# Sliding-window attention and a squared-ReLU feed-forward on one core: the first token group's down product formed as seven quarter products, with a new order of the whole program

## The chip, the core and the metric

The kernel runs on one NeuronCore of one Trainium2 chip. The metric is the device time of one execution in microseconds (us), smaller is better. The engines run beside each other, each through its own list of instructions in order: TensorE (PE; PEld is its weight load), VectorE (DVE), ScalarE (ACT), GpSimd (POOL) and SyncE (SP). Transfers are issued by SP, ACT and POOL and carried by 16 DMA engines.

## What is computed

```python
# attention: batch 8, heads 8, 576 positions, head dim 64, causal window of 64
scores = (1 / sqrt(64)) * q @ k.T
scores = where((rel >= 0) & (rel < 64), scores, -1e9)
attn = exp(scores - max) / (sum + 1e-9)
x = (attn @ v)  arranged as 4608 tokens x 512
# feed-forward: w_in 512 x 2048, w_out 2048 x 512
h = maximum(x @ w_in, 0)
out = (h * h) @ w_out
```

Inputs and output are 32-bit floats; on the chip the matrices are held as 16-bit floats and sums are formed in 32 bits.

## The kernel before

**Work and tiles.** Attention goes by tiles of 128 queries, 36 in all (0 to 35; the last four, 32 to 35, are the tails of two batches each). Four tiles make a group of 512 tokens, and there are nine groups. For a tile, the words of the program are: `fk`, `fq`, `fv` fetch (SP issues, 256 KB each), `kc`/`qc` or `kp`/`qp` and `vc` cast to 16 bits, `vl`/`vh` copy half tiles of v to a second layout, `T` (or `Ta`, `Tb`) transpose on TensorE with `ck`, `cq` copying the result out (tiles 0 to 7), or `tk`, `tq` transpose by DMA (tiles 8 on), `S` scores, `e` exponential on ACT, `m` mask on DVE, `V` the product with v, `n` normalization on DVE, `X` with `x` (or `dx` by DMA) the transpose of the result. `SS`, `VV` do two tiles.

**Feed-forward.** A group's hidden layer has 16 blocks of 128 columns. Groups 1 to 8 compute one block by `P` (UPm, L513: 4 matmuls 128x512), group 0 by `U` (L480: 8 matmuls 128x256, two blocks for half the tokens). Each is followed by a ReLU on ACT (`R`, `r`, L495) and a square (`Q`, `s`), whose last figure names the engine: 2 is ACT (L506), 1 is DVE (L510).

**Down product.** Groups 1 to 8 use seven products of quarters instead of eight (out_seven, L662): the hidden layer is cut by tokens and by blocks in four quarters, w_out likewise, and sums of quarters are multiplied. `hs` g.i.half forms the sums of the hidden layer on DVE (L676, 8 per group, 128x1024), `ws` kind.k the sums of w_out (L521, 16 once, on DVE, into `wb_all` and, kind 3, into w_out itself), `Z` g.n.half is half a product (8 matmuls 128x256, L696), `ev` g.n takes a product out of PSUM: n = 0 on ACT (L728), n = 1 to 6 on DVE (L730). Products 0 and 1 share a PSUM bank, 3 and 5, and 4 and 6; `sd` stores. Group 0 alone uses the plain form: `O` ts.fq, 4 matmuls 128x512 (L647), four such for each of four token tiles, `oe` copies out (two on ACT, two on DVE), `st` stores:

```python
    def O(ts, fq):
        if fq == 0:
            ops_of[ts] = psum_of("out")
        for f in range(4 * fq, 4 * fq + 4):
            nc.tensor.matmul(
                ops_of[ts][:], h2s[0][:, f, ts * P:(ts + 1) * P], w_out_sb[:, f, :],
                start=(f == 0), stop=(f == FFC - 1))
```

**Weights.** `fw` j loads a quarter of the columns of w_in (L203), `fo` j a quarter of the rows of w_out (L208). Both are issued by POOL, cast to 16 bits under way, and stand in POOL's list between its casts. Blocks 4j to 4j+3 use quarter j of both: `U` p.f2 needs quarter f2 // 2 of w_in; product 0 of the seven needs rows 0 and 1 of the quarters of w_out (half 0 the first, half 1 the second), product 1 quarters 2 and 3, and `ws` kind.0 and kind.1 quarters 0 and 2, kind.2 and kind.3 quarters 1 and 3.

**The order.** No scheduler places anything: the string ORDER (L16) lists some 1,270 words, and each engine gets its instructions in that order, with waits only where data or buffers ask for them. `W` n puts n matmuls on zeros into TensorE's list (L350, results unused). Buffers that matter: 14 stage buffers for fetched tiles, two PSUM banks called up (`ps_u`) and two called out (`ps_o`), which `U` takes in turn, `P` from up, `O` and `Z` from out; two buffers for the hidden layer (one group each), one `hs_all` for two of the four sums.

Of the kernel before, what the change touches and what calls it, by code (L numbers as in the profile page):

```python
# [33 lines left out]
fq13 r1.9 VV4 s1.9.2 qp12.0 P1.12 fv13 r1.2 n8 st3 O1.2 s1.2.1 r1.12 fk14 s1.12.2 hs1.0.0 X8 fq14
P1.4 x8.2 vc12.0 n9 P1.7 vh12.0 r1.4 hs1.1.0 s1.4.2 O1.3 kp13.0 h10 r1.7 tk12 hs1.2.0 Z1.0.0 oe1.2
s1.7.1 SS5 fv14 hs1.0.1 qp13.0 Z1.0.1 e11 st1 hs1.1.1 Z1.2.0 fk15 vc13.0 ev1.0 m11 fq15 e10 vl13.0
Z1.1.0 hs1.2.1 vh13.0 Z1.1.1 tq12 hs1.3.0 kp14.0 X9 ev1.1 Z1.2.1 m10 qp14.0 fv15 x9.2 hs1.3.1
Z1.3.0 fk16 ev1.2 VV5 Z1.4.0 n10 vc14.0 Z1.4.1 n11 vh14.0 X10 vl14.0 X11 x10.1 Z1.3.1 kp15.0 x11.1
P2.7 tk14 ev1.3 qp15.0 P2.10 ev1.4 r2.7 fq16 s2.7.2 SS6 r2.10 P2.8 fv16 e12 vc15.0 s2.10.1 Z1.5.0
tq14 vl15.0 r2.8 m12 P2.4 e13 kp16.0 s2.8.1 fk17 Z1.5.1 r2.4 m13 fq17 s2.4.2 P2.6 ev1.5 qp16.0 h14  # L40
P2.2 sd1.0 r2.6 fv17 s2.6.2 P2.11 vc16.0 fk18 r2.2 vh16.0 VV6 r2.11 P2.0 s2.2.2 s2.11.1 n12 P2.13
r2.0 kp17.0 n13 s2.0.2 P2.3 tk16 qp17.0 r2.13 SS7 r2.3 s2.13.1 dx12 Z1.6.0 e14 s2.3.1 P2.15 e15
m14 fq18 P2.5 vc17.0 r2.15 m15 tq16 s2.15.2 vl17.0 P2.1 r2.5 vh17.0 VV7 s2.5.2 fv18 kp18.0 P2.12
r2.1 n15 fk19 s2.1.2 P2.9 n14 r2.12 Z2.0.0 s2.12.1 r2.9 dx14 s2.9.1 Z2.0.1 qp18.0 hs2.0.0 fq19
Z1.6.1 ev2.0 hs2.2.0 P2.14 fv19 ev1.6 SS8 r2.14 hs2.1.0 vc18.0 sd1.1 Z2.1.0 e16 fk20 vh18.0
s2.14.1 Z2.2.0 fq20 kp19.0 e17 hs2.0.1 vl18.0 Z2.1.1 hs2.1.1 tk18 P3.14 hs2.2.1 ev2.1 qp19.0 fv20
m17 Z2.3.0 r3.14 tq18 m16 s3.14.2 P3.1 vc19.0 hs2.3.0 vl19.0 VV8 r3.1 fk21 hs2.3.1 Z2.2.1 fq21
s3.1.1 Z2.3.1 n16 kp20.0 P3.5 ev2.2 qp20.0 P3.0 ev2.3 r3.5 n17 s3.5.2 Z2.5.0 r3.0 h18 dx16 P3.12
s3.0.2 vc20.0 P3.11 r3.12 fv21 vh20.0 s3.12.1 Z2.4.0 fk22 r3.11 s3.11.1 Z2.5.1 kp21.0 P3.8 ev2.5
tk20 SS9 qp21.0 r3.8 P3.10 s3.8.2 tq20 e18 P3.9 r3.10 Z2.4.1 m18 sd2.0 vc21.0 s3.10.2 fq22 P3.2  # L50
r3.9 vh21.0 ev2.4 e19 vl21.0 P3.7 fv22 kp22.0 r3.2 m19 Z2.6.0 s3.2.2 VV9 r3.7 s3.9.2 P3.3 n19
s3.7.2 P3.13 n18 r3.3 s3.3.2 P3.6 dx18 r3.13 hs3.0.0 SS10 r3.6 s3.13.1 qp22.0 Z3.0.0 fk23 e20
s3.6.1 fq23 P3.4 e21 vc22.0 hs3.1.0 Z2.6.1 vl22.0 m20 r3.4 vh22.0 s3.4.1 P3.15 ev2.6 Z3.0.1 r3.15
hs3.2.0 sd2.1 Z3.2.0 fv23 kp23.0 ev3.0 m21 fk24 P4.13 s3.15.1 qp23.0 tk22 hs3.0.1 VV10 r4.13 P4.4
n20 s4.13.2 fq24 P4.9 hs3.2.1 r4.4 fv24 s4.4.2 n21 Z3.1.0 tq22 r4.9 vc23.0 hs3.1.1 P4.6 s4.9.2
vl23.0 hs3.3.0 fk25 P4.2 r4.6 kp24.0 fq25 s4.6.1 Z3.1.1 r4.2 h22 s4.2.2 P4.15 dx20 hs3.3.1 ev3.1
P4.10 qp24.0 r4.15 fv25 s4.15.2 Z3.3.0 fk26 vc24.0 r4.10 Z3.3.1 vh24.0 s4.10.2 P4.0 P4.7 r4.0
kp25.0 s4.0.2 SS11 tk24 r4.7 qp25.0 Z3.2.1 s4.7.2 P4.12 fq26 e23 ev3.2 P4.5 ev3.3 e22 tq24 m23
vc25.0 Z3.5.0 r4.5 m22 vh25.0 s4.5.2 fv26 Z3.5.1 kp26.0 r4.12 fk27 VV11 vl25.0 ev3.5 s4.12.2 P4.8
n22 sd3.0 fq27 Z3.4.0 n23 r4.8 qp26.0 Z3.4.1 s4.8.1 dx22 P4.11 ev3.4 fv27 P4.3 r4.11 vc26.0 fk28  # L60
s4.11.2 P4.14 vl26.0 r4.3 kp27.0 SS12 s4.3.2 vh26.0 P4.1 tk26 e25 Z3.6.0 r4.1 m25 fq28 s4.1.2
Z3.6.1 qp27.0 e24 hs4.0.0 Z4.0.0 tq26 ev3.6 r4.14 Z4.0.1 m24 fv28 Z4.3.0 hs4.1.0 vc27.0 ev4.0
sd3.1 fk29 s4.14.1 vl27.0 Z4.1.0 fq29 kp28.0 hs4.0.1 P5.7 hs4.3.0 VV12 r5.7 hs4.2.0 Z4.1.1 s5.7.1
# [779 lines left out]
```

## Time and profile before

| what | us |
|---|---|
| median of 3 runs | 296.81 (294.68, 296.81, 300.88) |
| the profiled execution, its own time | 295.67 |
| its span, first to last instruction | 294.0 |
| PE busy | 282.1 (96%) |
| DVE busy | 195.6 (67%) |
| ACT busy | 192.0 (65%) |
| POOL busy | 106.1 (36%) |

All steps below refer to the one profiled execution. A row of the groups gives line, engine, operation, tiles and shapes, how many, the busy time in all, the mean of one in ns, and the idle time before them with what ended it. Matmuls overlap: a mean of 379 ns is from issue to result, while the starts of two 128x512 matmuls are 216 ns apart, so the chain of work, which counts from start to start, is the better price of one. A timeline row gives start, duration and instruction.

### The profile page before, as it was taken

The page shows a single profiled execution, that of the slowest core. Times are in us where ns is not written, and L with a number is a line of the kernel's source. Part 1 is how long each engine was busy: PE and PEld are TensorE (multiplying, and loading weights), DVE is VectorE, ACT ScalarE, POOL GpSimd, SP SyncE. Part 2 cuts the span into 40 slices and gives each one's busy share as a digit, 9 for nine tenths or more (in the row PEclk, how much of TensorE's full clock was granted, in tenths as well). Part 3 has the DMA queues.
Part 4 walks back from the last instruction along what each step waited for, and adds up shares of the span by engine and source line. Part 5 has one row for each costly group of instructions (what it writes and reads, how often), then busy time and mean ns, then how long its engine had stood idle before and what let it go on. Part 6 is the DMA issues. An engine that isn't in the chain of part 4 may idle for free.

```text
span 294.0 us, 7221 instructions
## 1 busy us (share of the span) xinstructions
PE 282.1 (96%) x2894; PEld 185.3 (63%) x2894; DVE 195.6 (67%) x350; ACT 192.0 (65%) x311; POOL 106.1 (36%) x162
## 2 busy tenths in 40 slices
PE   8789799999989999999999999999999999999994
...
PEclk9989999999999999999999999999999999999999
DMA  7999999599999999998999998999999904401024
GB/s 220 303 258 253 203 197 196 120 252 227 214 226 195 256 169 257 197 248 184 219 242 225 195 227 161 228 215 172 261 197 281 231 18 109 78 31 71 2 93 121
DMA packets 162592, 55.51 MB, mean 189 GB/s; under 512 B 149248, under 2 KB 158464, under 8 KB 162560
## 3 DMA queue, kind: packets, MB, share of 16 engines
...
q10 hardware_dynamic: 1632, 0.79, 0.9%
...
q14 instruction: 10, 0.08, 0.1%
...
## 4 chain that ended last, share of the span: by engine, by line
PE 58%; DVE 0%; issue 0%; DVEq 0%
PE ps_u L516 27%; PE ps_o L696 26%; PE att L441 2%; PE att L416 2%; PE ps_u L696 1%; DVE u L730 0%; DVE osb_all L730 0%; DVEq L730 0%
## 5 line engine op out<-in xcount | busy, mean ns | idle before, releaser
L516 PE MATMUL ps_u<-xT,w_in_sb 128*128 128x512 f16 x512 | 123.2, 379 | 0.1
L495 ACT ACTIVATE hrelu<-ps_u 128x512 f32<-128x512 f32 x136 | 80.3, 593 | 60.5 <-PE ps_u L516 56.9
L516 PEld LDWEIGHTS <-w_in_sb 128*128 128x128 f16 x512 | 48.7, 98 | 46.4 <-issue 0.6
L696 PEld LDWEIGHTS <-h 128*128 128x128 f16 x640 | 62.0, 98 | 16.8 <-issue 1.7
L506 ACT ACTIVATE h<-hrelu 128x512 f16<-128x512 f32 x89 | 55.7, 630 | 2.3
L510 DVE SCALAR_TENSOR_TENSOR h<-ps_u,hrelu 128x512 f16<-128x512 f32 x51 | 34.9, 687 | 19.3 <-ACT hrelu L495 19.0
L696 PE MATMUL ps_o<-w_out_sb,h 128*128 128x256 f16 x368 | 46.2, 273 | 0.2 <-DVE u L730 0.2
L262 POOL CAST v_ev<-v_st 128x512 f16<-128x512 f32 x31 | 21.5, 694 | 51.6 <-DMA v_st<-in_v_dram 44.8
L423 ACT ACTIVATE pm<-att 128x1024 f16<-128x1024 f32 x36 | 35.8, 1020 | 3.5 <-PE att L416 3.5
L262 POOL CAST k<-k_st 128x512 f16<-128x512 f32 x32 | 22.3, 699 | 29.0 <-DMA k_st<-in_k_dram 26.5
L428 DVE TENSOR_TENSOR pm<-pm,mask_inner 128x1024 f16<-128x1024 f16 x28 | 22.3, 801 | 15.4 <-ACT pm L423 15.2
L696 PE MATMUL ps_o<-wb_all,h 128*128 128x256 f16 x240 | 30.6, 273 | 0.9 <-DVE u L730 0.9
L262 POOL COPY v_od<-v_ev 64x512 f16<-64x512 f16 x40 | 28.5, 714 | 6.4 <-ACT v_ev L260 3.3
L262 POOL CAST q<-q_st 128x512 f16<-128x512 f32 x28 | 19.5, 697 | 30.7 <-DMA q_st<-in_q_dram 30.5
L696 PEld LDWEIGHTS <-hs_all 128*128 128x128 f16 x256 | 24.7, 98 | 5.1
L448 DVE TENSOR_TENSOR x_sb<-att,rden 128x512 f16<-128x512 f32 x36 | 24.9, 692 | 1.2
L730 DVE SCALAR_TENSOR_TENSOR osb_all<-ps_o,u 128x512 f32<-128x512 f32 (+1 forms) x24 | 16.0, 667 | 12.3 <-PE ps_o L696 12.2
L696 PE MATMUL ps_o<-wb_all,hs_all 128*128 128x256 f16 x128 | 16.3, 273 | 0.0
L441 PEld LDWEIGHTS <-pm 128*64 128x64 f16 x576 | 11.2, 111 | 8.0 <-issue 3.6
L696 PE MATMUL ps_o<-w_out_sb,hs_all 128*128 128x256 f16 x128 | 16.1, 273 | 0.0
L647 PE MATMUL ps_o<-w_out_sb,h 128*128 128x512 f16 x64 | 15.3, 379 | 0.0
L676 DVE TENSOR_TENSOR hs_all<-h 128x1024 f16<-128x1024 f16 x16 | 12.2, 761 | 3.8 <-ACT h L506 3.5
...
## 6 DMA issues: line engine op xcount, KB each, us to landing
...
```

The lines of the kernel that those rows point to most:

```text
L262: (nc.gpsimd, nc.vector)[e].tensor_copy(out=dst, in_=src)
L423: nc.scalar.activation(out=pms[i][:, part], in_=scs[i][:, part], func=AF.Exp, scale=1.0 / float(D) ** 0.5)
L428: nc.vector.tensor_tensor(out=pms[i][:, part], in0=pms[i][:, part], in1=mask[:].rearrange("p (o a) b r -> p o (a b r)", o=1) .to_broadcast ...
L441: nc.tensor.matmul(avs[i][64 * blk:64 * blk + 64, h // 4, h % 4, 0:65], pms[i][:, h % 2, h0:h0 + 64], vv[:, h, 0:65], start=True, stop=True)
L448: nc.vector.tensor_tensor(out=x_of(i)[:, :, i % 2, :].rearrange("p (a b) (c d) -> p a b c d", a=2, c=2), in0=avs[i][:, :, :, 0:D].rearrang ...
L495: nc.scalar.activation(out=hr_of[key][:], in_=src, func=AF.Relu)
L506: nc.scalar.activation(out=dst, in_=hr, func=AF.Square)
L510: nc.vector.scalar_tensor_tensor(out=dst, in0=hps, scalar=0.0, in1=hr, op0=ALU.max, op1=ALU.mult)
L516: nc.tensor.matmul(hps, w_in_sb[:, c, f * P:(f + 1) * P], xT_of(g)[:, :, c, :], start=(c == 0), stop=(c == DMC - 1))
L647: nc.tensor.matmul(ops_of[ts][:], h2s[0][:, f, ts * P:(ts + 1) * P], w_out_sb[:, f, :], start=(f == 0), stop=(f == FFC - 1))
L696: nc.tensor.matmul(banks[bank][m], a[:, kk, m * P:(m + 1) * P], w[:, kk], start=(first and kk == 0 and (m == 0 or split(bank))), stop=(kk ...
L730: nc.vector.scalar_tensor_tensor(out=dst, in0=src, scalar=OUT_SCALE, in1=other, op0=ALU.mult, op1=ALU.add)
```

## The change

Group 0's down product goes by the same seven products as the others: the words `O`, `oe`, `st` of group 0 (16, 4 and 4) are gone, and 14 `Z0`, 8 `hs0`, 7 `ev0` and 2 `sd0` come in. The whole order is a new one: the words of all groups stand in other places, some squares and copies change engine (squares `s` on ACT 71 instead of 78, on DVE 57 instead of 50), and there are 47 matmuls on zeros instead of 30, all of them ahead of the first words of group 1. One fetch (`fq1`) moves from SP's list to ACT's. On POOL, `fw0` and `fw1` stand next to each other, and the third load of w_out (`fo2`) stands ahead of `qp8`, the fourth (`fo3`) behind `vc8` and `vh8`. `fetch_w_in` can load part of a quarter (`fx`), which no word of the order uses: there are four `fw` before and after. Line numbers after grow by two.

```diff
 ORDER = '''
-W8 ct cp fq0 cd fv0.1 fk0 fq1 fq2 cm fk1 fk2 qc0.0 fk3 Tb0 W8 vc0.1 fk4 cq0.2 vh0.0 fq3 kc0.0 fq4
...
-Q0.2.2 T5 W1 vl5.0 x3.1 vh5.2 qc6.1 U1.3 fw2 vc6.2 ck5.1 T6 vh6.0 cq5.2 U1.0 vl6.2 kc7.0 qc7.1
-R1.3 U1.2 fw3 fq8 ck6.2 vc7.1 T7 R1.0 h6 vl7.0 U1.1 R1.2 ck7.1 cq6.2 Q1.0.1 Q1.2.2 S6 W1 cq7.1 e6
-S7 e7 S5 W1 m6 fv8 kp8.0 e5 V6 W1 m7 Q1.3.2 V7 W2 fo0 m5 R1.1 n7 U0.4 fo1 Q1.1.1 U1.5 R0.4 n6 fk9
-qp8.0 Q0.4.2 U1.4 R1.5 X7 R1.4 V5 x7.1 fo2 U1.6 n5 Q1.4.2 U0.7 Q1.5.1 R1.6 Q1.6.2 U0.6 R0.7 fo3 X5
-R0.6 X6 x5.1 U1.7 Q0.6.2 U0.5 x6.2 Q0.7.2 P1.0 R1.7 R0.5 Q1.7.1 O0.0 r1.0 Q0.5.2 fq9 P1.1 vc8.0
-s1.0.2 vh8.0 P1.11 r1.1 s1.1.2 O0.1 r1.11 P1.15 s1.11.2 P1.8 r1.15 ws0.0 s1.15.2 O2.0 ws1.0 r1.8
-O2.1 ws0.1 fv9 s1.8.2 kp9.0 ws1.1 P1.3 tk8 qp9.0 ws2.0 P1.5 r1.3 ws0.2 fk10 O2.2 s1.3.1 r1.5 vc9.0
-fq10 ws1.2 O0.2 vl9.0 ws0.3 tq8 vh9.0 O0.3 ws1.3 O2.3 oe0.1 fv10 ws2.3 P1.14 fk11 oe2.2 ws2.1
-kp10.0 st2 O3.0 r1.14 s1.5.1 fq11 O3.1 s1.14.1 qp10.0 ws2.2 fv11 P1.6 st0 SS4 fk12 r1.6 O3.2 e8
...
+W8 ct cp fk0 cd fv0.1 fq0 fq1.1 fq2 fk1 cm fk2 fk3 kc0.0 fk4 Ta0 W7 vc0.0 fq3 ck0.2 vh0.1 fq4
+qc0.1 Tb0 W2 qc1.1 fv1 cq0.1 Tb1 W1 fv2 cq1.1 S0 W3 kc1.0 e0 qc2.1 Tb2 kc2.2 Ta1 W2 m0 kc3.2 cq2.1
+gk3 fw0 V0 ck1.2 n0 Ta3 fw1 qc3.2 S1 Ta2 W2 ck3.1 kc4.2 qc4.0 e1 ck2.1 Ta4 W1 fv3 Tb4 W1 h2 ck4.2
...
+T5 W1 kc6.0 vc5.2 ck5.1 X3 vl5.2 vh5.0 X4 W1 x3.1 x4.2 cq5.1 fw2 U1.2 vc6.2 qc6.1 fw3 S5 vl6.1
+R1.2 T6 vh6.1 kc7.0 e5 U1.0 qc7.1 Q1.2.1 fq8 ck6.2 T7 vc7.1 R1.0 U1.3 ck7.1 Q1.0.2 vl7.0 U1.1
+cq6.2 cq7.1 R1.3 m5 S7 W1 Q1.3.2 fv8 kp8.0 h6 V5 W3 e7 n5 R1.1 S6 m7 X5 W3 e6 x5.2 V7 W2 m6 Q1.1.2
+fo0 n7 V6 U0.4 n6 fo1 X7 R0.4 fk9 U1.4 x7.1 fo2 Q0.4.2 X6 U0.5 R1.4 qp8.0 x6.1 Q1.4.1 U1.7 R0.5
+Q0.5.2 U1.5 fq9 vc8.0 R1.7 vh8.0 P1.8 R1.5 Q1.7.1 fo3 Q1.5.2 U0.7 r1.8 hs0.0.0 U0.6 R0.7 s1.8.1
+Q0.7.2 U1.6 hs0.2.0 R0.6 P1.1 R1.6 Q0.6.1 Q1.6.2 hs0.1.0 P1.0 r1.1 hs0.0.1 s1.1.2 P1.4 r1.0 Z0.0.0
+hs0.2.1 s1.0.2 r1.4 P1.12 hs0.1.1 fv9 kp9.0 s1.4.2 P1.11 r1.12 tk8 s1.12.2 P1.6 ws0.1 r1.11 Z0.0.1
+fk10 r1.6 ws1.1 fq10 s1.11.2 P1.14 ws0.0 ev0.0 qp9.0 ws1.0 P1.15 s1.6.2 tq8 ws3.1 r1.14 vc9.0
+Z0.1.0 r1.15 ws3.0 vh9.0 fv10 s1.15.2 s1.14.1 Z0.1.1 vl9.0 fk11 ws0.2 P1.5 ev0.1 ws2.0 kp10.0 P1.7
+ws1.2 r1.5 ws0.3 qp10.0 Z0.2.0 r1.7 s1.5.1 s1.7.2 ws1.3 P1.9 hs0.3.1 P1.3 r1.9 ws3.3 fq11 vc10.0
+s1.9.2 SS4 ws2.3 vh10.0 r1.3 P1.2 fv11 ws2.1 e9 vl10.0 s1.3.1 Z0.2.1 kp11.0 e8 m9 fk12 P1.13
...
-    def fetch_w_in(quar):
-        cols = slice(quar * FQ, (quar + 1) * FQ)
+    def fetch_w_in(quar, parts=1, part=0):
+        n = FQ // parts
+        cols = slice(quar * FQ + part * n, quar * FQ + part * n + n)
```

More of the change, by code (lines that the diff above doesn't have):

```diff
@@ L34 @@
[L34 to L63, printed above, removed]
@@ new lines @@
+fk10 r1.6 ws1.1 fq10 s1.11.2 P1.14 ws0.0 ev0.0 qp9.0 ws1.0 P1.15 s1.6.2 tq8 ws3.1 r1.14 vc9.0
+Z0.1.0 r1.15 ws3.0 vh9.0 fv10 s1.15.2 s1.14.1 Z0.1.1 vl9.0 fk11 ws0.2 P1.5 ev0.1 ws2.0 kp10.0 P1.7
+ws1.2 r1.5 ws0.3 qp10.0 Z0.2.0 r1.7 s1.5.1 s1.7.2 ws1.3 P1.9 hs0.3.1 P1.3 r1.9 ws3.3 fq11 vc10.0
+s1.9.2 SS4 ws2.3 vh10.0 r1.3 P1.2 fv11 ws2.1 e9 vl10.0 s1.3.1 Z0.2.1 kp11.0 e8 m9 fk12 P1.13
+qp11.0 tk10 ws2.2 r1.2 Z0.3.0 ws3.2 s1.2.2 vc11.0 fq12 r1.13 hs0.3.0 Z0.3.1 vl11.0 s1.13.2 ev0.2
+kp12.0 P1.10 fv12 m8 tq10 Z0.4.0 r1.10 ev0.3 s1.10.2 Z0.4.1 hs1.0.1 fk13 Z0.5.0 h10 fq13 hs1.0.0
@@ new lines @@
+qp12.0 Z0.5.1 ev0.4 VV4 vc12.0 ev0.5 Z0.6.0 vh12.0 n8 sd0.0 fv13 Z1.0.0 n9 fk14 Z1.0.1 hs1.2.0
+kp13.0 X9 tk12 ev1.0 hs1.2.1 X8 Z0.6.1 qp13.0 x9.2 hs1.1.0 x8.2 Z1.1.0 fq14 ev0.6 SS5 hs1.3.0 fv14
+Z1.2.0 e11 sd0.1 hs1.1.1 vc13.0 Z1.1.1 fk15 e10 vl13.0 m11 fq15 Z1.2.1 ev1.1 kp14.0 m10 Z1.4.0
+vh13.0 tq12 ev1.2 hs1.3.1 VV5 fv15 Z1.4.1 qp14.0 n10 fk16 Z1.3.0 n11 vc14.0 X10 vh14.0 X11 x10.1
+Z1.3.1 x11.2 vl14.0 P2.6 ev1.3 P2.8 ev1.4 kp15.0 r2.6 s2.6.2 P2.10 tk14 qp15.0 r2.8 Z1.6.0 r2.10
+s2.8.1 fq16 s2.10.2 P2.13 fv16 SS6 r2.13 vc15.0 tq14 P2.7 e13 s2.13.1 vl15.0 Z1.5.0 kp16.0 r2.7
@@ new lines @@
+Z2.3.1 vh18.0 hs2.3.0 kp19.0 hs2.3.1 Z2.4.0 tk18 ev2.3 P3.11 m17 qp19.0 P3.12 r3.11 fk20 vc19.0
+s3.11.1 Z2.5.0 tq18 r3.12 vl19.0 s3.12.1 P3.1 fq20 P3.0 r3.1 fv20 s3.1.1 Z2.5.1 r3.0 h18 s3.0.2
+P3.14 ev2.5 kp20.0 P3.8 sd2.0 r3.14 fk21 s3.14.2 VV8 fq21 r3.8 P3.15 n16 qp20.0 Z2.4.1 s3.8.1
+r3.15 n17 vc20.0 s3.15.2 P3.9 vh20.0 ev2.4 dx16 SS9 r3.9 Z2.6.0 e19 s3.9.1 fv21 P3.4 e18 m19 fk22
+kp21.0 P3.3 r3.4 tk20 m18 qp21.0 s3.4.2 P3.5 r3.3 tq20 VV9 r3.5 P3.7 s3.3.2 n19 s3.5.2 fq22 P3.6
+n18 vc21.0 r3.7 vh21.0 Z2.6.1 s3.7.1 r3.6 dx18 kp22.0 s3.6.1 P3.2 vl21.0 ev2.6 fv22 P3.10 r3.2
@@ new lines @@
+fk23 s3.2.2 P3.13 sd2.1 r3.10 fq23 Z3.0.0 r3.13 s3.10.1 SS10 qp22.0 hs3.0.0 fv23 Z3.0.1 e21
+hs3.2.0 Z3.3.0 ev3.0 hs3.1.0 e20 P4.6 m21 vc22.0 Z3.1.0 s3.13.1 vl22.0 r4.6 hs3.0.1 s4.6.2 kp23.0
+P4.15 vh22.0 m20 tk22 P4.13 r4.15 hs3.1.1 s4.15.2 Z3.3.1 fk24 hs3.3.0 r4.13 qp23.0 Z3.1.1 fq24
+s4.13.2 hs3.2.1 P4.8 hs3.3.1 ev3.1 vc23.0 tq22 Z3.2.0 vl23.0 r4.8 s4.8.1 fv24 VV10 fk25 P4.12 n21
+kp24.0 Z3.2.1 n20 r4.12 s4.12.2 qp24.0 P4.7 ev3.2 dx20 P4.5 ev3.3 r4.7 h22 fq25 s4.7.2 Z3.5.0 r4.5
+vc24.0 Z3.5.1 fv25 s4.5.2 vh24.0 P4.1 ev3.5 kp25.0 sd3.0 SS11 r4.1 tk24 Z3.4.0 e22 s4.1.1 P4.10
```

81 lines of the change are left out of this document (44 added, 37 removed).

## The prediction, made before the changed kernel ran

> **What bounds the kernel now.** I read the page first (engines, slices), then the chain that ended last, the timelines of PE, DVE, ACT and POOL, what PE waited for, busy time by stretch, and the landings of transfers. The page, engines and slices:
>
> ```profile
> PE 282.1 (96%) x2894; PEld 185.3 (63%) x2894; DVE 195.6 (67%) x350; ACT 192.0 (65%) x311; POOL 106.1 (36%) x162
> ...
> PE   8789799999989999999999999999999999999994
> ...
> PEclk9989999999999999999999999999999999999999
> DMA  7999999599999999998999998999999904401024
> ```
>
> PE is the bound from about 37 us on. Before that it has gaps, with the DMA engines full. The chain, from start to start (start, length, what):
>
> ```profile
> 145.21 0.87 PE ps_o L696 x8
> 146.08 1.73 PE ps_u L516 x8
> ```
>
> These are my prices: eight matmuls of 256 columns, one `Z`, 0.87 us; four of 512, one `P`, 0.865. PE's timeline (start, length, idle time before in brackets):
>
> ```profile
> 36.94 1.04 PE L484 MATMUL ps_u<-xT,w_in_sb 128*128 128x256 f16 x8
> ...
> 51.12 1.89 PE L647 MATMUL ps_o<-w_out_sb,h 128*128 128x512 f16 x8
> 52.85 1.89 PE L516 MATMUL ps_u<-xT,w_in_sb 128*128 128x512 f16 x8
> ...
> 61.58 0.64 PE L416 MATMUL att<-qT,kT 64*128 64x64 f16 x32
> ...
> 83.07 1.91 PE L696 MATMUL ps_o<-wb_all,h 128*128 128x256 f16 x16 [0.89 <-DVE u L730]
> ```
>
> `U0.4` starts at 36.94. From there to 289.97, PE stops twice for DVE (0.89 and 0.24). Eight matmuls of `O` take 52.85 - 51.12 = 1.73, so an `O` is 0.865. POOL's timeline shows when w_out is asked for (L209), and the casts of q8 and v8 beside it:
>
> ```profile
> 31.74 1.48 POOL L209 DMA_DIRECT2D w_out_sb<-in_moe_w_out_dram  x2
> 40.15 0.61 POOL L262 CAST q<-q_st 128x512 f16<-128x512 f32 x1 [6.93 <-DMA q_st<-in_q_dram]
> 40.70 1.48 POOL L209 DMA_DIRECT2D w_out_sb<-in_moe_w_out_dram  x2
> 46.79 0.61 POOL L262 CAST v_ev<-v_st 128x512 f16<-128x512 f32 x1 [4.62 <-DMA v_st<-in_v_dram]
> 47.47 0.61 POOL L262 COPY v_od<-v_ev 64x512 f16<-64x512 f16 x1
> ```
>
> And busy time by stretch (busy, with instructions in brackets; granted clock, DMA share, GB/s): ACT is nearly full in the first, DVE in the second.
>
> ```profile
> 40.00:50.00 10.00, 10.00 (x87) 6.84 (x86) 3.00 (x6) 9.50 (x18) 3.25 (x5) 1.00 1.20 196
> 70.00:80.00 10.00, 10.00 (x104) 6.98 (x103) 9.86 (x15) 7.36 (x12) 5.81 (x9) 1.00 1.06 224
> ```
>
> **The change part by part.**
>
> *Products of group 0.* 16 `O` x 0.865 = 13.84 go, 14 `Z` x 0.87 = 12.18 come. PE is the bound there, so this is **-1.7**.
>
> *The head (to `U0.4`).* The order is new, so I walked it with before's durations. Tiles 0 to 4 go about as before. The stretch ends with tile 7, whose q lands late: DVE waited for it until 28.73. After that, in the new lists: cast to 29.3, transposes, kT copy, then qT copy to 31.8; `S7` 31.9; ACT reaches `e7` at 32.5 and, behind a ReLU, `e6` at 34.35, ending 35.35; mask `m6` to 36.1; `V6` 36.2; `U0.4` at about 36.75. The 17 added matmuls on zeros (17 x 0.216 = 3.7) lie in gaps of this walk, where PE waits for copies and exponentials; were all that cover gone they would cost the 3.7. Moving `fq1` to ACT's list, idle there until 5.0, spares SP one issue of 0.63 ahead of `fk1`; landings are limited by the full DMA engines, so I take 0 (from -0.6). After `U0.4`, `V5` (0.33) and `X5` (0.23) are no longer to be done. Together -0.2 - 0.55 = **-0.7**. Ends: -3.5 (q7's own chain of cast 0.58, transposes 0.45, copies 1.36, scores 0.3, exponential 0.93, mask 0.72, V 0.33 is 4.7, so `U0.4` not before 33.4) and +2 (DMA or ACT late by three exponentials).
>
> *Last quarter of w_out.* `fo3` was issued at 41.4. Now it stands behind `vc8` and `vh8`, which ended at 48.1. Its readers: `Z0.1.1`, and on DVE `ws0.2`, behind which stand `ev0.1` and `s1.5.1` (a PSUM bank for `P1.9`). PE reaches `Z0.1.1` about 55.0 (`U0.4` at 36.75, then 8 `U`, 2 `X`, 9 `P` and 3 `Z`: 17.8 by the prices, and 0.4 while ACT, at 1.2 for a block's ReLU and square, frees banks). The eight loads of weights took 6.4 to 14.4 us to land; those that met an empty queue of their kind (issued 9.9 and 27.2) 6.4 and 8.1. So landing is 54.5 to 62.5, nearest 54.5 to 56.2, as `fo2`, now ahead of `qp8`, leaves the queue at about 50. I take **+0.3**, ends 0 and +7.5. The Trainium skill, page "DMA: Bandwidth & Descriptors", section "Anatomy of one DMA — SWDGE (gpsimd) path", fits 2.0 us plus bytes over 436 GB/s: by it 1 MB read takes an estimated 4.4 us, the load lands at 52.5 and this term is 0. The trace disagrees (6.4 to 14.4 beside other traffic), and the rows decide.
>
> *Scores of tiles 8 and 9 (`SS4`).* PE would be there at 60.5; q8's transpose, issued 56.70, lands 4.0 later. Its fetches stay in their order, so I take 60.7: **+0.2** (0 to +1.5, if `fo3` takes bandwidth from k9 and q9).
>
> *DVE.* New: 8 `hs` x 0.79 = 6.3, 6 `ev` x 0.69 = 4.1; less two `oe`, 1.4. By the words, from `P1.1` to `VV5`, DVE has 33 us of work against 33.8 on PE; in before between the same words it had 26 against 34.5. It also waits for w_out in that stretch (before: 4.9 on `wb_all`). So DVE lags PE and banks come free late, around `Z1.2` to `Z1.4` at 76 to 82. Before paid 0.89 there; walking DVE's list I find a lag of 0.5 to 2 us. **+0.7** more than before; ends -0.9 (no stall is left) and +4. The row behind the doubt: sums at L676 took 0.69 alone and 1.03 to 1.09 beside POOL's copies (73.97 to 81.32). The skill's page "SBUF — State Buffer", section "Who interferes with whom", says that a DVE instruction with two SBUF inputs and a GpSimd one that reads SBUF exclude each other; those rows agree, and the new sums stand beside POOL's casts of tiles 8 to 10.
>
> *Squares moved from ACT to DVE*, seven `s` and one `Q`: off the chain elsewhere (PE never waited after 118.8); 0, ends ±1. *ACT in 37 to 57*: 17.8 us of work against 18.7 on PE, so no more than the 0.4 above. *w_in's quarters loaded whole*: both kernels issue four loads of 512 KB; 0. *SP's list.* Four `st` go and two `sd0` come, with the same bytes. `sd0.0` waits for `ev0.5`, at 71 by my walk, and ahead of `fv13`, `fk14` and tiles 12 and 13's transposes; before, SP came to `fv13` at 72.64: 0, ends 0 and +1. *The half clock* (granted 0.50 in 14 to 16 us): more matmuls on zeros may remove it; PE waits for copies there, so 0. *The tail* after PE's last matmul (294.0 - 289.97 = 4.0) keeps its order: 0.
>
> Sum: -1.7 - 0.7 + 0.3 + 0.2 + 0.7 = -1.2. The profiled execution, span 294.0, own time 295.67, becomes 292.8 and 294.5. It stands 1.1 under the runs' median of 296.81; from that the sum is 295.6. I give **295.0**.
>
> **Rivals.**
>
> *The late quarter of w_out decides (slower).* Place: `Z0.1.1` and `ws0.2`. Price: landing minus 55.0. It ends the gain when the landing is 1.5 us later than I took it, at 56.8, and at 14.4 after 48.1, 62.5, it costs 7.5: 295.0 - 0.3 + 7.5 = 302.2. For it: POOL's own wait of 4.62 for v8, by which `fo3` moves later still if v8 is late. Against: its queue is nearly empty by then.
>
> *DVE becomes the bound from 46 to 82.* With each of the 8 new sums at 1.09 rather than 0.79 (2.4) and waits for w_out that are not made up, PE waits 4 us in place of 0.7: 298.3. For it: 9.86 of 10 in 70 to 80 already before. Against: after 82 it has slack, and PE waited 0.89 only.
>
> *The head shrinks.* q7 lands sooner, since fetches issue earlier, and `U0.4` starts at 33.4 to 34: 295.0 - 3 = 292.0, with no stall left in DVE 290.4. Against: the DMA share is over 1.0 from 12 us on, with the same bytes.
>
> *It does nothing that counts.* The head is held by transfers and the 1.7 is lost at `SS4`: 296.5, inside the forecast's range.
>
> **How the numbers follow.** Forecast 0.58 (own range 293 to 297.5), late w_out 0.14, DVE bound 0.15, shorter head 0.13. The range 291.3 to 300.5 reaches into the three others and leaves out about 0.08 below and 0.11 above. Two per cent of 296.81, about what a measurement of this kernel can tell from no change, is 290.9 to 302.7. Below it: half of the shorter heads, 0.07. Above: most of the late w_out, with more than its own stall, 0.10, and 0.04 of DVE bound. Within: 0.79.
>
> **What would show it.** In the profile after: `Z0` at 0.87 each, no L647 (first step); `U0.4` at 36 to 37.5 (head); L211's fourth issue near 48 and PE's idle time at `Z0.1.1`, with DVE's `wb_all` wait (w_out); PE's wait at 60 to 61 on qT; PE's waits on L732 at 76 to 82 below 2 us (DVE); PE without waits after 90. I am wrong if `U0.4` starts before 35 or after 39, if PE stands still over 3 us between 45 and 82, or if new waits appear behind 90 us, where the new order was not walked.

## The result, and the profile after

| | before | after |
|---|---|---|
| median of 20 executions each, us | 295.91 | 294.75 |
| lowest to highest | 294.68 to 300.88 | 293.86 to 296.06 |
| the profiled execution, own time | 295.67 | 295.40 |
| its span | 294.0 | 293.6 |
| start of `U0.4` | 36.94 | 38.33 |
| end of PE's last matmul | 289.97 | 289.53 |

The ratio of after to before is 0.9963, 95% interval 0.9946 to 0.9980: 1.2 us less by the medians of the table and 1.1 by the ratio, a small gain that is clear of the noise, within 2%. Executions more than 1.5% above the fastest of their kernel (one of before's 20 here, five of its 80 and one of the first experiment's 12 below) are left out of the ratios and of the counts of executions. The forecast was 295.0: right by the sum, not by its terms. The profiled execution of after is one of its slower ones (295.40 against 294.75), so the pair of profiles shows only 0.3 to 0.4 us.

The page of after, engines and slices:

```profile
PE 283.8 (97%) x2959; PEld 190.5 (65%) x2959; DVE 211.8 (72%) x368; ACT 187.5 (64%) x304; POOL 108.0 (37%) x162
...
PE   7989799999999999999999999999999999999994
...
PEclk9999999999999999999999999999999999999999
```

PE is the bound as before. The 8 in the third slice of PEclk is gone: in this execution no stretch at half clock is left. The chain of after (start, length, what):

```profile
119.25 0.87 PE ps_o L698 x8
120.12 1.73 PE ps_u L518 x8
```

A `Z` is 0.87 and a `P` 0.865, as in the prices. PE's timeline of after, from the last scores of the head to the rows that the prediction named:

```profile
32.14 0.41 PE L418 MATMUL att<-qT,kT 64*128 64x64 f16 x16
32.48 0.39 PE L363 MATMUL att<-zero 128*128 128x512 f16 x1
...
34.04 0.81 PE L363 MATMUL att<-zero 128*128 128x512 f16 x3 [0.79 <-ACT pm L425]
34.78 0.20 PE L418 MATMUL att<-qT,kH 64*128 64x64 f16 x2
...
35.12 0.40 PE L461 MATMUL att<-ident,x_sb 128*128 128x128 f16 x4
36.30 0.81 PE L363 MATMUL att<-zero 128*128 128x512 f16 x3 [0.79 <-ACT pm L425]
37.04 0.22 PE L443 MATMUL att<-v_od,pm 128*64 128x65 f16 x1
...
37.42 0.61 PE L363 MATMUL att<-zero 128*128 128x512 f16 x2
...
38.33 1.05 PE L486 MATMUL ps_u<-xT,w_in_sb 128*128 128x256 f16 x8
...
55.56 1.91 PE L698 MATMUL ps_o<-w_out_sb,h 128*128 128x256 f16 x16
...
61.73 0.64 PE L418 MATMUL att<-qT,kT 64*128 64x64 f16 x32
...
66.26 1.03 PE L698 MATMUL ps_o<-w_out_sb,hs_all 128*128 128x256 f16 x8 [0.31 <-DVE w_out_sb L535]
...
84.46 0.40 PE L461 MATMUL att<-ident,x_sb 128*128 128x128 f16 x4 [0.38 <-DVE x_sb L450]
```

Two things are to be read here. First, the matmuls on zeros (L363) write to `att`, the bank that the scores or products behind them will use, and they themselves wait 0.79 us for ACT to have read it. Only when the three are through do `S6` (34.78) and `V7` (37.04) follow. Second, behind `U0.4` PE waits 0.31, 0.38 and (at 117.36) 0.15 for DVE, 0.84 in all, against 1.13 before; `Z0.1.0` and `Z0.1.1` run at 55.56 without a wait for w_out, and `SS4` at 61.73 without one for qT. ACT's timeline of after shows what the zeros waited for:

```profile
32.98 1.01 ACT L425 ACTIVATE pm<-att 128x1024 f16<-128x1024 f32 x1
...
35.23 1.02 ACT L425 ACTIVATE pm<-att 128x1024 f16<-128x1024 f32 x1 [0.75 <-PE att L418]
```

The first is `e7`: it frees the bank into which the zeros ahead of `S6` go. The second is `e6`, which waits 0.75 for `S6`, and so for those zeros; it frees the bank that the zeros ahead of `V7` want. There are two such banks, taken in turn by `S7`, `V5`, `S6`, `X5`, `V7`, `V6`, so each delay is handed on. POOL's timeline of after:

```profile
46.79 0.62 POOL L264 CAST v_ev<-v_st 128x512 f16<-128x512 f32 x1 [6.98 <-DMA v_st<-in_v_dram]
47.47 1.17 POOL L264 COPY v_od<-v_ev 64x512 f16<-64x512 f16 x1
48.59 0.75 POOL L211 DMA_DIRECT2D w_out_sb<-in_moe_w_out_dram  x1
```

The last quarter is asked for at 48.6, as forecast, and its time to landing, 5.8 us, is the least of the four loads of w_out (median 11.8, most 16.1); it is there by 54.4, ahead of PE. And the stretches in which DVE was feared (busy of PE, PEld, DVE, ACT, POOL; clock, DMA share, GB/s):

```profile
60.00:70.00 10.00, 9.69 (x96) 6.46 (x95) 9.49 (x15) 7.50 (x12) 7.06 (x10) 1.00 0.88 199
70.00:80.00 10.00, 10.00 (x149) 8.70 (x147) 9.38 (x16) 3.76 (x6) 4.80 (x8) 1.00 0.92 217
```

DVE is 9.49 and 9.38 of 10 busy there, and PE stands still for 0.31.

### The profile page after: what moved, and what is told of

It reads as the page before. It is cut to its first block, busy times and chain, and to the rows that moved or that the text cites. A ratio compares the mean times of both kernels' runs of the same rounds, so it can differ in the third digit from the quotient of the medians.

```text
span 293.6 us, 7350 instructions
## 1 busy us (share of the span) xinstructions
PE 283.8 (97%) x2959; PEld 190.5 (65%) x2959; DVE 211.8 (72%) x368; ACT 187.5 (64%) x304; POOL 108.0 (37%) x162
## 3 DMA queue, kind: packets, MB, share of 16 engines
q10 hardware_dynamic: 1904, 1.05, 1.2%
## 4 chain that ended last, share of the span: by engine, by line
PE 59%; DVE 1%; issue 0%
PE ps_u L518 28%; PE ps_o L698 25%; PE att L443 2%; PE att L418 2%; PE ps_u L698 1%; DVE h L678 0%; DVE h L512 0%; DVE u L732 0%; DVE pm L430 0%; DVE osb_all L732 0%
## 5 line engine op out<-in xcount | busy, mean ns | idle before, releaser
L698 PEld LDWEIGHTS <-h 128*128 128x128 f16 x720 | 69.6, 98 | 16.9 <-issue 0.4
L512 DVE SCALAR_TENSOR_TENSOR h<-ps_u,hrelu 128x512 f16<-128x512 f32 x61 | 41.8, 688 | 32.0 <-ACT hrelu L497 31.4
L508 ACT ACTIVATE h<-hrelu 128x512 f16<-128x512 f32 x81 | 50.6, 629 | 4.9 <-PE ps_o L698 2.8
L698 PE MATMUL ps_o<-w_out_sb,h 128*128 128x256 f16 x416 | 51.7, 273 | 0.0
L264 POOL COPY v_od<-v_ev 64x512 f16<-64x512 f16 x41 | 30.9, 753 | 13.2 <-ACT v_ev L262 9.0
L698 PE MATMUL ps_o<-wb_all,h 128*128 128x256 f16 x272 | 35.3, 273 | 0.0
L264 POOL CAST v_ev<-v_st 128x512 f16<-128x512 f32 x30 | 21.2, 708 | 37.5 <-DMA v_st<-in_v_dram 32.4
L698 PEld LDWEIGHTS <-hs_all 128*128 128x128 f16 x288 | 27.8, 98 | 7.0 <-issue 0.5
L698 PE MATMUL ps_o<-w_out_sb,hs_all 128*128 128x256 f16 x144 | 18.3, 273 | 0.3 <-DVE w_out_sb L535 0.3
L698 PE MATMUL ps_o<-wb_all,hs_all 128*128 128x256 f16 x144 | 18.5, 273 | 0.0
L678 DVE TENSOR_TENSOR hs_all<-hs_all,h 128x1024 f16<-128x1024 f16 x18 | 15.2, 847 | 0.2
## 6 DMA issues: line engine op xcount, KB each, us to landing
w_out_sb<-in_moe_w_out_dram POOLq DMA_DIRECT2D x4, 512.0 KB, 11.8
```

Of the source, the lines that this page charges most:

```text
L264: (nc.gpsimd, nc.vector)[e].tensor_copy(out=dst, in_=src)
L508: nc.scalar.activation(out=dst, in_=hr, func=AF.Square)
L512: nc.vector.scalar_tensor_tensor(out=dst, in0=hps, scalar=0.0, in1=hr, op0=ALU.max, op1=ALU.mult)
L678: (nc.gpsimd, nc.vector)[e].tensor_tensor(out=Sh[i][:, ks], in0=x[:, ks], in1=y[:, ks], op=op)
L698: nc.tensor.matmul(banks[bank][m], a[:, kk, m * P:(m + 1) * P], w[:, kk], start=(first and kk == 0 and (m == 0 or split(bank))), stop=(kk ...
```

## The experiments

Each set of four kernels ran on one chip beside the kernel before; ratios are to that one. Times are medians, to be set against 294.75 of after, or ratios against its 0.9963. The medians of before in the three sets are 296.24, 296.07 and 295.88 (295.91 beside after), so a few tenths between medians of different sets say nothing.

**Undo the head: before's words as far as `U0.4`, after's behind it.**

```
-(after's words ahead of U0.4)
+(before's words ahead of U0.4)
 U0.4 [+Q1.1.1] ... [+V5] x7.1 [+n5] ... [+X5] x6.1 [+x5.1] ...
```

> The head of the order before (all words up to U0.4) in front of the rest of the new order, with V5, n5, X5, x5 and Q1.1 put into the rest. Theory: the new head is worse, since U0.4 starts at 38.33 instead of 36.94; here it starts at 36.9 again, PE gets 0.55 us more to do behind it, and the time is 294.75 - 1.39 + 0.55 = 293.9. Rival: what holds the kernel behind the head is landings (w_out, q8), so PE waits for them and the time stays at 294.7 or goes up.

294.63, ratio 0.9946 (0.9921 to 0.9970): as after, within the intervals. `U0.4` starts at 35.92, not at the 36.94 that was expected: these are before's words, but this execution has no half clock (its first `U` starts at 18.64, that of before's profile at 19.52). So everything that the change gains over before is in what follows the head; the new head itself brings about nothing. The theory's 293.9 is met only by the five of its 11 executions whose mean granted clock is 0.995 or more (median 293.95); the other six have 295.06. What that clock does comes up again below.

**The product alone, in before's order.** `Z0`, `hs0` and `ev0` stand where `O`, `oe` stood.

```
-O0.0 ... O0.1 ... O2.0 ... O2.1 ...
+Z0.0.0 ... Z0.0.1 ev0.0 ... Z0.1.0 ...
```

> The order before, with group 0's O replaced by Z0 in place, and hs0, ev0, sd0 and earlier ws3 put in by hand; nothing else is moved, 30 matmuls on zeros stay. Theory: the products are worth 1.7 us on PE and the rest of the new order little, so 295.9 - 1.7 = 294.2. Rival: without a new order the added DVE work (10.4 us, 1.4 taken out) holds PSUM banks, and PE waits 1 to 4 us more between 45 and 85: 295.2 to 298.

298.03, ratio 1.0074 (1.0046 to 1.0102): slower than before. The longest of eight waits of PE (timeline of this kernel):

```profile
62.24 1.02 PE L515 MATMUL ps_u<-xT,w_in_sb 128*128 128x512 f16 x4 [1.36 <-DVE h L509]
```

The eight are 4.5 us in all, and seven of them are for DVE. The fear that DVE becomes the bound was well founded for the old order; in the new one PE waits 0.84. This profile, whose words as far as `U0.4` are before's, shows one thing more (granted clock third from the end):

```profile
13.00:15.00 2.00, 1.32 (x25) 0.96 (x25) 1.05 (x4) 2.00 (x3) 1.92 (x3) 1.00 1.17 193
15.00:17.00 2.00, 1.33 (x37) 0.90 (x36) 1.91 (x5) 1.98 (x4) 0.00 (x0) 1.00 1.25 253
36.00:38.00 2.00, 2.00 (x19) 1.13 (x14) 1.61 (x4) 0.09 (x1) 0.00 (x0) 0.50 1.21 194
```

The half clock, which before's profile has between 13 and 17 us, is here between 36 and 38.

**The other way round: after's order with the `O` products of before.**

```
-Z0.0.0 ... Z0.0.1 ... Z0.1.0 ... (and hs0, ev0, sd0)
+O0.0 ... O0.1 ... O0.2 ... (and oe, st; ws3 late)
```

> The new order with group 0's plain product put back: 16 O in the places of 14 Z0, no hs0 and ev0, ws3 behind the last O that reads what it changes. Theory: 294.75 + 1.7 = 296.4, since PE is the bound there. Rival: the saved DVE work pays for it, 295 or less.

297.23, ratio 1.0040 (1.0016 to 1.0063): 2.3 to 2.5 above after. 1.66 is the 16 `O` against 14 `Z`; PE's waits behind `U0.4` are 1.44 (0.99, 0.30 and 0.15) against 0.84. Together that is 2.26.

**Without the nine zeros between `S7` and `U0.4`.**

```
-S7 W1 ... V5 W3 e7 ... S6 m7 X5 W3 e6 x5.2 V7 W2 m6 ... V6 U0.4
+S7 ... V5 e7 ... S6 m7 X5 e6 x5.2 V7 m6 ... V6 U0.4
```

> The new order without the matmuls on zeros between S7 and U0.4 (9 of 47). Theory: they write to the PSUM bank that the next real work takes, so they stand behind the same wait (PE waits 0.79 twice for an exponential ahead of them) and then delay S6, e6, V7 and V6: U0.4 starts 1.0 to 1.6 us sooner, and the time is 293.2 to 293.8. Rival: they lie in waits and cost nothing (294.75), or PE's granted clock falls to 0.50 for a stretch without them and the time rises to 295 or more.

293.84, ratio 0.9931 (0.9909 to 0.9954), about 0.9 below after; the two intervals overlap by a little. PE's timeline:

```profile
33.63 0.20 PE L416 MATMUL att<-qT,kH 64*128 64x64 f16 x2 [0.96 <-ACT pm L423]
...
35.24 0.19 PE L441 MATMUL att<-v_od,pm 128*64 128x65 f16 x1 [0.88 <-ACT pm L423]
...
36.25 1.60 PE L484 MATMUL ps_u<-xT,w_in_sb 128*128 128x256 f16 x8
...
38.07 1.91 PE L484 MATMUL ps_o<-xT,w_in_sb 128*128 128x256 f16 x8
```

`S6` comes 1.15 earlier than in after, `V7` 1.8, `U0.4` 2.08; 0.4 of each is there before the zeros already (the `U` at 27.21 in after starts at 26.81 here). But `U0.4` and the next `U`, eight matmuls each, which took 1.05 and 1.04 in after, now take 1.60 and 1.91. Stretches of this kernel (granted clock third from the end):

```profile
36.00:38.00 2.00, 2.00 (x28) 1.59 (x27) 1.47 (x3) 0.21 (x2) 0.61 (x1) 0.65 1.22 203
38.00:40.00 2.00, 2.00 (x14) 1.47 (x13) 0.42 (x1) 1.11 (x2) 0.00 (x0) 0.50 1.22 196
```

The half clock is back, right where PE has become the bound. Five of nine executions have a mean clock under 0.995 (median 294.60), the other four do not (293.57). Theory and rival each hold in part: the zeros delay the head, and they keep the clock; the two groups of executions are 1.0 apart.

**The nine zeros kept, but with nothing to wait for.** They write into the bank of `U0.4`, free there.

```
-S7 W1 ... V5 W3 e7 ... X5 W3 e6 x5.2 V7 W2 m6
+S7 w1 ... V5 w3 e7 ... X5 w3 e6 x5.2 V7 w2 m6
+    def warm_early(n, kind):
+        if kind not in held:
+            held[kind] = psum_of(kind)
+        for _ in range(n):
+            nc.tensor.matmul(held[kind][:], zero[:, 0:P], zero[:], start=True, stop=True)
...
+        elif verb == "w":
+            warm_early(*args, "any")
```

> The changed kernel, and the nine matmuls on zeros between S7 and U0.4 write into U0.4's own PSUM bank, free since U1.2 was read, rather than into the bank of the scores or products behind them; so they wait for nothing. Theory (the head lost time because the nine stood behind e7 and e6, not because they take PE's time): they now lie in PE's two idle stretches there; S6 starts at about 34.0 in place of 34.8, U0.4 at 36.4 to 36.9 in place of 38.33, at full granted clock; the time falls by 1.4 to 1.9 us, to about 293.1, some 0.7 below the kernel without the nine (293.84). Rival (the nine cost their own length, 9 x 0.216 = 1.9, wherever they stand): U0.4 at 38 or later, 294.7. Rival (time was lost to the early start's transfers: the third quarter of w_in isn't there yet): U0.4 waits for it, about 294.

293.53, ratio 0.9902 (0.9866 to 0.9938), 1.2 below after by the medians and 1.8 by the ratios. PE's timeline:

```profile
32.99 0.82 PE L357 MATMUL ps_u<-zero 128*128 128x512 f16 x3
...
34.43 0.81 PE L357 MATMUL ps_u<-zero 128*128 128x512 f16 x3
...
35.47 0.19 PE L450 MATMUL att<-v_od,pm 128*64 128x65 f16 x1 [0.23 <-ACT pm L432]
...
36.76 1.05 PE L493 MATMUL ps_u<-xT,w_in_sb 128*128 128x256 f16 x8
```

The same nine matmuls now run while PE would stand still, the eight of `U0.4` take 1.05, and `U0.4` starts at 36.76, where the walk of the prediction had put it (36.75). That the two agree to 0.01 is luck, since `U0.4` moves by some 0.6 between profiles of the same head. But the steps agree too: `e6` runs from 34.30 to 35.32 (walk: 34.35 to 35.35), and only `e7`, at 32.79, is 0.3 later than in the walk. So what was wrong in it was the place where the zeros wait. The other two rivals fall: the nine do not cost their length, and w_in's third quarter is there. Against the kernel without the nine the median is 0.3 lower, not the 0.7 that was expected, and the four executions of that kernel at full clock have 293.57: what the nine give in their free bank is the clock, which all six executions keep.

**No zeros between the first 15 and `S7`.** The 14 words hold 23 matmuls on zeros (15, 23 and 9 make the 47; the 22 in the expectation is a miscount).

```
-Tb0 W2 ... Tb1 W1 ... S0 W3 ... Ta1 W2 ... T6 (14 words W)
+Tb0 ... Tb1 ... S0 ... Ta1 ... T6
```

> The changed kernel without the 22 matmuls on zeros that stand behind the first 15 and ahead of S7. Theory (as predicted: PE waits for copies there, so the granted clock counts for nothing): the granted clock falls to 0.50 for one stretch of some 3 us in the first 20 us, as in the kernel before, the transposes and scores in it take longer, and U0.4 stays within 0.4 us of 38.33, because tile 7's q lands when it lands; time within 0.4 us of 294.75. Rival (PE is on the path of the first tiles): the first U starts 0.7 us or more later than 18.78 and U0.4 0.5 to 1.5 us later than 38.33; time 295.3 to 296.3.

295.82, ratio 0.9978 (0.9942 to 1.0014): 1.0 above after by the medians but 0.4 by the ratios, and its interval takes in the whole of after's, so the time alone decides nothing between theory and rival. Its profiled execution is one of the three of twelve that kept the clock, so the profile says little: `U0.4` at 37.49, first `U` at 18.26, no worse than in after (38.33 and 18.78). The clock over the span says more: below 0.995 in 9 of 12 executions, with a median of 296.18, against 294.40 for the three others; in after it is below in 2 of 20. So the zeros keep the clock, and whether it falls without them varies from execution to execution, which neither theory nor rival had.

**Before, with nine zeros more ahead of its first `U`.**

```
-Ta0 ... Tb1 ... S0 ... Ta2 ... Ta4
+Ta0 W2 ... Tb1 W1 ... S0 W3 ... Ta2 W2 ... Ta4 W1
```

> The kernel before, with nine more matmuls on zeros ahead of the first U, in a bank that is idle there. Theory (most executions of before have a stretch at half the granted clock in the first tiles, and it costs; the new order's zeros took it away): the granted clock over the span is 0.997 or more in nearly all executions (29 of 47 of before were below), and the median is 0.3 to 0.8 below before's. Rival (the price of the half clock is nil, as predicted, PE waiting for copies there): the clock rises and the time stays within 0.2 of before's. Rival (zeros delay the transposes behind them): 0.3 or more above before's.

295.33, ratio 0.9983 (0.9958 to 1.0009). Stretches 13 to 15 and 15 to 17 of before, ahead of those of this kernel:

```profile
13.00:15.00 2.00, 1.80 (x28) 1.40 (x29) 1.94 (x6) 1.61 (x3) 0.81 (x2) 0.62 1.23 204
15.00:17.00 2.00, 1.95 (x39) 1.30 (x37) 1.44 (x4) 1.79 (x4) 0.00 (x0) 0.53 1.26 268
```

```profile
13.00:15.00 2.00, 1.80 (x41) 1.07 (x40) 1.94 (x6) 1.41 (x3) 0.60 (x1) 1.00 1.23 202
15.00:17.00 2.00, 1.22 (x37) 0.81 (x31) 1.64 (x5) 1.99 (x4) 0.00 (x0) 1.00 1.25 258
```

The first `U` of before, then the first `U` and `U0.4` of this kernel (PE's timelines):

```profile
19.52 1.03 PE L484 MATMUL ps_u<-xT,w_in_sb 128*128 128x256 f16 x8 [0.55 <-DVE xT L262]
```

```profile
18.50 1.03 PE L482 MATMUL ps_u<-xT,w_in_sb 128*128 128x256 f16 x8
...
35.93 1.04 PE L482 MATMUL ps_u<-xT,w_in_sb 128*128 128x256 f16 x8
```

The clock is full, here and in 11 of 12 executions (0.995 or more over the span). Of 75 executions of before in the three sets, 29 have that; their median is 295.31, that of the 46 others 296.26. This kernel's 295.33 is the first of these. Its ratio to before includes 1, and the 27 executions of before in its own set have a median of 295.45, so the time does not show that the zeros gain anything; by that alone the rival, a price of nil, could hold. The profiles speak against it. With the same words but for the zeros, the first `U` is 1.0 earlier here, and `U0.4`, at 35.93 against 36.94, is still 1.0 earlier. The first experiment, at full clock without added zeros, has 18.64 and 35.92, and the product alone, at full clock up to there, has its first `U` at 18.70. (Between profiles of after's head at full clock the first `U` varies from 18.20 to 18.91.) So the half clock in the first tiles delays the head, by 0.8 to 1.0 in before's profile. It is not the only place. The kernel with the product alone has it at 36 to 38 behind before's words, and before's executions fall into three groups: 29 at 0.995 or more, 27 at 0.991 to 0.994 (median 296.03), and 19 under 0.990 (296.68). As an estimate from these means, 0.993 over 294 us is some 4 us at half clock, 0.987 some 8, so that many executions have two stretches; none of the 19 was profiled.

**The head alone: after's words as far as `U0.4`, before's order and `O` products behind it.**

```
 (after's words ahead of U0.4)
-U0.4 (after's words, Z0)
+U0.4 (before's words without Q1.1.1, V5, n5, X5, x5.1; O)
```

> The changed kernel's head as far as U0.4, and behind it the order and the 16 O products of the kernel before. Theory (the zeros' wait for the scores' banks ate what the new head gives): U0.4 at about 38.3 and full granted clock; against before's executions -0.55 for V5 and X5 that are done, -0.5 for the clock, +1.4 for U0.4, so 0.1 to 0.6 above before's median. Rival (the head as forecast): 0.5 to 1 below before's median.

296.12, ratio 1.0006 (0.9978 to 1.0033), `U0.4` at 38.31. The theory holds by `U0.4` and by the medians; the interval, from 0.65 below before to 1.0 above, does not by itself exclude the upper end of the rival. At full clock (11 of its 12) the median is 296.06, 0.75 above before's 295.31. The first experiment at full clock (5 of its 11) has 293.95, 1.4 below (1.7 below the nine of its own set, 295.68). The two add up to -0.6 (-1.0), and after at full clock (18 of 20) is at 294.65, -0.7.

**w_out's last quarter still later.** `fo3` behind `vh9`.

```
-... Q1.7.1 fo3 Q1.5.2 ... vh9.0 fv10 ...
+... Q1.7.1 Q1.5.2 ... vh9.0 fo3 fv10 ...
```

> The changed kernel, and the load of w_out's last quarter stands five GpSimd words later, behind vh9, so that it is issued at about 53.7 in place of 48.6. Theory (the rival of the prediction, its price the landing minus the time that PE reaches Z0.1.1, 55.56): landing 5.8 behind the issue, 59.5; PE waits 3.9 at Z0.1.1, and the time rises by 3.5 to 4, to 298.5. Rival (DVE and ACT, 1 to 2 us behind PE there, use the wait to catch up, and the waits for DVE that follow go): not over 2.5 us, 297. Rival (the load lands in 4.4 as it meets an empty queue of its kind): PE waits 2.5, 297.2.

300.91, ratio 1.0152 (1.0109 to 1.0196): 6.2 above after by the medians, 5.6 by the ratios. PE's timeline, then the stretches:

```profile
55.07 1.04 PE L696 MATMUL ps_o<-w_out_sb,h 128*128 128x256 f16 x8
60.83 1.87 PE L696 MATMUL ps_o<-w_out_sb,h 128*128 128x256 f16 x8 [4.72 <-DMA w_out_sb<-in_moe_w_out_dram]
62.49 2.43 PE L516 MATMUL ps_u<-xT,w_in_sb 128*128 128x512 f16 x8
```

```profile
60.00:61.00 1.00, 0.17 (x2) 0.11 (x2) 0.12 (x1) 0.00 (x0) 0.00 (x0) 0.57 1.31 192
61.00:62.00 1.00, 1.00 (x6) 0.75 (x5) 1.00 (x4) 0.00 (x0) 0.00 (x0) 0.50 1.36 101
62.00:63.00 1.00, 1.00 (x6) 0.54 (x4) 0.31 (x1) 0.27 (x1) 0.02 (x1) 0.50 1.28 288
63.00:64.00 1.00, 1.00 (x5) 0.41 (x4) 0.00 (x0) 0.33 (x1) 0.94 (x2) 0.72 1.28 293
```

Issued at 52.01, the load landed 8.8 later, not 5.8 or 4.4. PE waited 4.72, and then eight matmuls of `Z` took 1.87 in place of 1.04: the clock was at half when the wait ended, and stayed so to about 63.6, some 2.7 us of work that lost 1.4. All three prices were too low: the landing was later, and none had the clock in it. 4.7 and 1.4 are 6.1. The Trainium skill, page "TensorE: Matmul & The Clock Gate", section "HAM oscillation — how this bites in real kernels", has as a rule that PE should have no idle gap over about 3.4 us. The 4.72 here agrees with it. Keeping to it was not enough in the kernel without the nine zeros, where the clock fell behind gaps of 0.96 and 0.88, and there the measurement decides.

**Four sums of group 0 done twice.**

```
-hs0.0.0 ... hs0.1.0 ... hs0.0.1 ... hs0.1.1
+hs0.0.0 hs0.0.0 ... hs0.1.0 hs0.1.0 ... hs0.0.1 hs0.0.1 ... hs0.1.1 hs0.1.1
```

> The changed kernel, with four of the eight sums of group 0's halves (hs0.0 and hs0.1, both halves) done twice, which changes no value: 2.7 to 3.2 us more on DVE between 44 and 52. Theory (DVE is not the bound from 46 to 82, and has idle time of about 3 us there, so an error of 3 us in its price costs little): PE's waits for DVE between 46 and 90 rise from 0.7 to 1 to 2.5; time 295 to 296.3. Rival (DVE is at its bound, so that what comes on top of it comes out at the end): all 2.7 to 3.2, 297.6. Rival (slack of more than 3 us, so that the prediction's fear had no ground at all): 0, 294.75.

295.83, ratio 0.9993 (0.9968 to 1.0017): 1.1 above after by the medians, 0.9 by the ratios, for about 3 more on DVE. PE's waits for DVE are 0.18, 0.17, 0.23, 0.35 and 0.46, spread from 48 to 172, 1.39 in all against 0.84. The time is the theory's, its place is not: between 46 and 90 the waits are 0.58, no more than in after (0.69), and half of the 1.1 is in no wait of this profile. What can be said is that 3 us more on DVE cost about a third of that.

**Seven squares of groups 4 and 5 back on ACT.**

```
-s4.8.1 s4.1.1 s4.10.1 s4.2.1 s5.0.1 s5.13.1 s5.1.1
+s4.8.2 s4.1.2 s4.10.2 s4.2.2 s5.0.2 s5.13.2 s5.1.2
```

> The changed kernel, with seven squares of groups 4 and 5 on ACT again rather than on DVE. Theory (predicted at nothing: behind 118 us neither engine makes PE wait): within 0.3 us of 294.75. Rival (ACT, at 0.60 for a square behind 0.59 for each ReLU, frees PSUM banks late, or DVE's freed 4.5 us were needed): PE gets waits between 140 and 200 or loses some; 0.5 us or more either way.

294.86, ratio 0.9962 (0.9941 to 0.9982), as after. PE has no wait between 140 and 200. Nothing hung on the engine of these seven squares.

**A version that beats both, tried further: `X5` and `V6` behind `U0.4`,** and seven zeros in `U0.4`'s bank.

```
-S7 w1 ... V5 w3 e7 ... S6 m7 X5 w3 e6 x5.2 V7 w2 m6 ... V6 U0.4 ...
+S7 w1 ... V5 w3 e7 ... S6 m7 V7 w3 e6 U0.4 m6 ... V6 ... X7 fk9 X5 U1.4 ...
```

> The changed kernel with the zeros in U0.4's own bank (seven of them left), X5 behind U0.4, and U0.4 ahead of V6. Theory (what ends the head is now e6, its mask and V6, which U0.4 doesn't need): V7 no longer waits for the bank that e6 frees, U0.4 starts at 35.7 to 36.0, V6 and X5 (0.33 and 0.23) come behind it; 0.2 to 0.5 us below the kernel with only the zeros moved (293.53), so about 293.2, and under it too the changed kernel by 1.5. Rival (the third quarter of w_in lands later than that): U0.4 waits for it until up to 36.5, 293.6 to 294.

293.48, ratio 0.9912 (0.9880 to 0.9944): no better than 293.53. PE's timeline:

```profile
35.36 1.04 PE L493 MATMUL ps_u<-xT,w_in_sb 128*128 128x256 f16 x8
...
37.81 0.40 PE L468 MATMUL att<-ident,x_sb 128*128 128x128 f16 x4 [0.70 <-DVE x_sb L457]
```

`U0.4` starts still 1.4 earlier and w_in is there; but `X5` now stands behind `V6` in the turn of the two banks, and waits 0.70 for the step that reads `V6`. The stall has moved by one word.

## Why the prediction was right, and what in it was wrong

The time was right by luck: a step that failed was made up for by others that had been priced too dearly, or at nothing. The 295.0 itself lies between two sums, 294.5 from the profiled execution and 295.6 from the median of three runs (296.81, where twenty have 295.91), and the prediction gives no reason for that place.

*Products of group 0, -1.7.* Right: `Z` at 0.87, no O left, and with `O` back in the same order the time is 2.3 to 2.5 higher, of which 0.6 is waits.

*The head, -0.7.* This step failed. The prediction said that the added zeros "lie in gaps of this walk, where PE waits for copies and exponentials". The gaps were there, but the nine behind `S7` could not lie in them: in the code's `warm` they take the bank of the word behind them, and so wait with it and run when the wait is over. That is in the code (L350), and I counted the zeros' time without asking what they wait for. `U0.4` came at 38.33, not 36.75: +1.4 less the 0.55 for `V5` and `X5` is +0.8 in place of -0.7, and the head alone measured +0.75 at full clock. (The two agree in part by chance. Before's profile has the half clock; its words at full clock put `U0.4` at 35.92 and 35.93, and five other kernels with the new head put it at 37.84 to 38.47, so that by profiles at full clock the head would be 1.4 to 2.0 worse.) With the same zeros in a free bank, `U0.4` is at 36.76: the rest of the walk (q7, copies, `e7`, `e6`, `m6`, `V6`) was right to 0.3.

*The half clock, 0.* Too small. "PE waits for copies there" is true of many rows between 8 and 18 us, but in before's profile, with the stretch, the first `U` is 0.8 to 1.0 and `U0.4` 1.0 later than in profiles without it, the executions of before with a mean clock under 0.995 are 0.9 longer in the median, and the change, which has nine zeros more ahead of its first `U` (31 against 22), has such a clock in 2 of 20 only. In the median of before that is worth 0.6 to 0.75 over all three sets together (0.5, 0.9 and 0.15 in the single ones). That the low clock makes the whole difference in time is argued: something else that varies, a late transfer say, could bring both, and no run takes the two apart. One profiled execution could not show that a low clock comes in 46 of 75, nor that a second place for it lies at 36 to 38.

*Last quarter of w_out, +0.3; `SS4`, +0.2.* Both 0: the landing took 5.8, less than any of the eight (6.4 to 14.4), and q8 was there. The mechanism is real, as the later load shows; it costs the wait, as the rival had it, and also the clock behind the wait, which it did not have.

*DVE, +0.7.* Measured -0.3 (waits of 0.84 against 1.13). The work that I added up was there (9.49 and 9.38 of 10); the lag of 0.5 to 2 us that I found by walking did not come out on PE. The order has to do with it: the same sums put into before's order cost 4.5 of waits. In after DVE even has idle time between its `hs0` (0.57, 0.33 and 1.22 for ACT between 44 and 56); that this is the reason is argued, not shown. The doubled sums put the slack there at about 2 of 3 us, an estimate from the time. (The row behind the doubt was read a little too evenly: of the sums from 73.97 to 81.32 one took 0.98 and one 0.68.)

*Squares, w_in, SP's list and the tail, 0:* nothing in the runs speaks against them; only seven of the eight squares were tested.

With the head at full clock these make -1.7, +0.8, -0.3 and about -0.7, so -1.9, where the times show -1.1 to -1.2. About 0.7 is not found. It lies behind `U0.4`: from there to the last matmul, waits taken off, after takes 250.36 and before 251.90, 1.5 less where the products, `V5` and `X5` should make 2.2. And it comes with the order, not with the products: the kernel with `O` back and the head alone have the same work on PE from `U0.4` on, in after's and in before's order, and take 252.1 and 251.1. Single profiles of one order differ by up to 0.8 (249.96 to 250.74 for after and four kernels that share its order from there), so the size is rough; what in the order costs it stays open.

*The rivals.* The late w_out and the DVE bound did not come, but each was one change of order away (300.91 and 298.03). The shorter head did not come either, nor the rival by which nothing counts (296.5). The forecast's own signs put `U0.4` at 36 to 37.5, and 38.33 came out wrong; so, by little, did "PE without waits after 90" (0.15 at 117.36). The chances do not fit each other: 0.14 above 302.7 cannot be more than the 0.11 above 300.5.
